# Attention over 128 heads on one core: engine programs rewritten as loops, and V's second unit multiplied one block later

## The chip, the core and the metric

The kernel runs on one core of a Trainium2 chip. A core has a matrix engine (TensorE, PE in the profile), a vector engine (VectorE, DVE), an activation engine (ScalarE, ACT), a general engine (GpSimd, POOL) and a queue engine for transfers (SyncE, SP), each with an instruction stream of its own; they meet only through semaphores. Sixteen DMA engines move data between HBM and the on-chip memory SBUF. Matmul results land in PSUM. The metric is the time of one execution on the device in microseconds (us), as the median of several runs.

## What is computed

Plain softmax attention with few queries and many keys, in bfloat16:

```python
B, H, Sq, Skv, Dh = 8, 16, 16, 2048, 256
scores = einsum('bhqd,bhkd->bhqk', q, k) * Dh ** -0.5
attn = softmax(scores)
out = einsum('bhqk,bhkd->bhqd', attn, v)
```

There are 128 heads (8 x 16), each with 16 queries and 2048 keys of 256 elements. K and V have 134 MB each, q and the output 1 MB each. Every byte of K and V is read once, so the kernel moves 270 MB.

## The kernel before, in words

**Blocks and units.** The 128 heads are taken in G = 16 blocks of 8 heads. A block has two units (e = 0 and 1) of K and two of V. A unit is 4 heads: 8192 rows of 256, laid out as 128 partitions x 64 rows x 256 elements, 4 MB, loaded with one DMA. SBUF holds four unit slots in the tensor `SL`, called KA, KB, VA and VB.

**Work of a block.** DVE transposes each K unit in place, in 32 x 32 squares of 4-byte words, so that the contraction lies on the partitions (`on_vector`, L154; four transposes a unit). PE then multiplies q with K: `qk` (L234 and L235, the helper `mm`; 16 matmuls of 512 columns for each half of a unit, 64 for a block) adds up scores of both units in the four PSUM banks of `S_ps`. The stationary operand is `QW`, a block-diagonal copy of the scaled queries that ACT writes for each block (`qwb`, L174). DVE takes the maximum over all 2048 scores (L156), ACT the exponentials in two halves with their sums (L206, into `P_sb`), DVE transposes these into `PTc` (L162, two halves) and computes the reciprocal of the sum (L164, L166). ACT copies `PTc` into `PTz` (L219), a tensor that is zero outside the diagonal squares: eight copies, four for each unit. PE multiplies `PTz` with V (`pv`, L251: 64 matmuls of 256 columns per unit, each with a weight load of its own), in a PSUM bank of its own for each unit. ACT evacuates each unit's 64 rows with the reciprocal as scale (`evac`, L180) and issues the store of the block's 128 output rows (L184).

**Order.** All loads go through SP (`load`, L97; the q load at L100), in the order K of block 0, K of block 1, V of block 0, K of block 2, V of block 1 and so on, K one block ahead of V. K of block 0 goes into the V slots, which are free then. A load of K waits until QK of the block before has read that slot (semaphores `c_qk`), a load of V until PV of the block before has (`c_pv`). PE runs in each round: QK of block g, then both PV units of block g-1; a wait on `c_cp` says that `PTz` of that block is written. ACT runs in each round: `QW` for the next block, the exponentials, evacuation and store of the block before last, then the eight copies. DVE runs K transposes, maximum, the transposes into `PTc`, sums, then the K transposes of the next block. At the end the last V units go into the K slots, in pieces that get smaller (`TAIL_A`, `TAIL`), so that PV can begin before the whole unit has landed.

**Programs.** PE's rounds 1 to 15 are one hardware loop whose body is written out (about 350 instructions with fixed addresses; only its semaphore thresholds come from the loop's register). The programs of SP, ACT and DVE are written out for all 16 blocks.

Of the kernel before, what the change touches and what calls it, by code (L numbers as in the profile page):

```python
# [7 lines left out]
PE = mybir.EngineType.PE  # L8
BF16 = mybir.dt.bfloat16
F32 = mybir.dt.float32  # L10

T = 64
KA, KB, VA, VB = 0, 1, 2, 3


def bass_standalone__softmax_full_bidir__sampling_kernel(
# [17 lines left out]
    qh = q.rearrange("b h s d -> (b h) (s d)")  # L34
    oh = out.rearrange("b h s d -> (b h s) d")

    with ExitStack() as es:
# [5 lines left out]
        PTc = ec(nc.sbuf_tensor("PTc", [128, T, 32], BF16))  # L43
        PTz = ec(nc.sbuf_tensor("PTz", [128, 2, T, 128], BF16))
        O_fin = ec(nc.sbuf_tensor("O_fin", [128, 2, D], BF16))
        negm = ec(nc.sbuf_tensor("negm", [128, G], F32))
        lsum = ec(nc.sbuf_tensor("lsum", [128, G, 2], F32))
        ltot = ec(nc.sbuf_tensor("ltot", [128, G], F32))
        rinv = ec(nc.sbuf_tensor("rinv", [128, G], F32))

        S_ps = ec(nc.psum_tensor("S_ps", [128, 4, 512], F32))
        O_ps = ec(nc.psum_tensor("O_ps", [128, 4, 512], F32))
# [4 lines left out]
        s_q = sem("s_q")  # L57
        s_k = [sem("s_ka"), sem("s_kb")]
        s_k0 = [sem("s_k0a"), sem("s_k0b")]
        s_v = [sem("s_va"), sem("s_vb")]  # L60
        s_st = [sem("s_st%d" % i) for i in range(2)]
        s_fin = sem("s_fin")
        c_pool = sem("c_pool")
        c_qt = sem("c_qt")
        c_qw = sem("c_qw")
        c_kt = [[sem("c_kt%d%d" % (e, h)) for h in range(2)] for e in range(2)]
        c_qk = [sem("c_qka"), sem("c_qkb")]
# [5 lines left out]
        c_pv = [sem("c_pv0"), sem("c_pv1")]  # L73
        c_pl = sem("c_pl")
# [4 lines left out]
        def ap_of(t_ap, offset, dims):  # L79
            return bass.AP(tensor=t_ap.tensor, offset=offset, ap=[list(t_ap.ap[0])] + [list(d) for d in dims])  # L80


        TAIL = [(0, 19), (19, 14), (33, 10), (43, 7), (50, 5), (55, 4), (59, 3), (62, 2)]
        TAIL_A = [(0, 37), (37, 27)]
        s_tail = [sem("s_t%d" % i) for i in range(len(TAIL))]
        s_vl = [sem("s_vl%d" % i) for i in range(len(TAIL_A))]
        s_vc = sem("s_vc")
        s_kl = sem("s_kl")

        def obank(g, e):  # L90
            return e + (2 if g == last else 0)

        def kslot(g, e):
            return (VA, VB)[e] if g == 0 else (KA, KB)[e]
# [3 lines left out]

        def on_sync(eng):
            eng.dma_start(QT[:], qh).then_inc(s_q, 16)  # L100
            for e in range(2):
                load(eng, ku, 0, e, kslot(0, e), 0, T, s_k0[e])
            for g in range(1, G):
                for e in range(2):
                    if g >= 2:
                        eng.wait_ge(c_qk[e], g)
                    if (g, e) != (last, 1):
                        load(eng, ku, g, e, kslot(g, e), 0, T, s_k[e])
                    else:
                        load(eng, ku, g, e, kslot(g, e), 0, 32, s_k[e])  # L110
                        load(eng, ku, g, e, kslot(g, e), 32, 32, s_kl)
                w = g - 1
                for e in range(2):
                    if w:
                        eng.wait_ge(c_pv[e], w)
                    else:
                        eng.wait_ge(c_qk[e], 1)
                    if (w, e) != (last - 1, 1):
                        load(eng, vu, w, e, (VA, VB)[e], 0, T, s_v[e])
                        if e:  # L120
                            eng.sem_inc(s_vc, 16)
                    else:
                        load(eng, vu, w, e, VB, 0, 32, s_v[e])
                        load(eng, vu, w, e, VB, 32, 32, s_vc)

            eng.wait_ge(c_qk[0], G)
            for (a, n), s in zip(TAIL_A, s_vl):
                load(eng, vu, last, 0, KA, a, n, s)
            eng.wait_ge(c_qk[1], G)
            for (a, n), s in zip(TAIL, s_tail):  # L130
                load(eng, vu, last, 1, KB, a, n, s)
            eng.wait_ge(c_ev, 2 * last + 2)
            eng.dma_start(oh[128 * last:128 * last + 128, :], O_fin[:, last % 2, :]).then_inc(s_fin, 16)
            eng.wait_ge(s_fin, 16)

        def on_gpsimd(eng):
            eng.memset(PTz[:].rearrange("p a t c -> p (a t c)").bitcast(F32), 0.0).then_inc(c_pool, 1)  # L137

        def on_vector(eng):
# [4 lines left out]
            for g in range(G):  # L144
                for e in range(2):
                    for c in range(4):
                        if g == 0 and c == 0:
                            eng.wait_ge(s_k0[e], 16)
                        elif c == 0:
                            eng.wait_ge(s_k[e], 16 * g)  # L150
                        elif (g, e, c) == (last, 1, 2):
                            eng.wait_ge(s_kl, 16)
# [5 lines left out]
                for h in range(2):  # L158
                    eng.wait_ge(c_ex[h], g + 1)
                    if g and h == 0:  # L160
                        eng.wait_ge(c_cp, 8 * g)
# [6 lines left out]
        def on_scalar(eng):  # L168
# [29 lines left out]
            for g in range(G):  # L198
# [4 lines left out]
                if g:  # L203
                    eng.wait_ge(c_pt, 2 * g)
# [113 lines left out]
```

## Time and profile before

| what | value |
|---|---|
| time, median of 3 runs | 636.18 us (635.99 to 636.28) |
| the profiled execution | 636.1 us, of which its span (first to last instruction) 634.8 us |
| DVE busy | 365.2 us (58%), of it K transposes 284.2 |
| ACT busy | 214.8 us (34%), of it copies to `PTz` 134.9 |
| HBM read and written | 269.48 MB and 1.05 MB |
| mean transfer rate over the span | 426 GB/s |
| chain that ended last, by engine | DMA 58%, PE 23%, DVE 16%, ACT 2% |
| granted TensorE clock, mean | 0.917 |

The profile is of one execution. Busy shares are means over the whole span; the 40 slices show how they change over time. The profile names each instruction by its engine and by its line in the kernel (L154 is line 154 of the listing above), its operation and its tiles. "Idle before, releaser" says how long an engine waited ahead of an instruction, and what it waited for. The DMA issues are listed by line, with the time from issue to landing.

### The profile page before, as it was taken

How to read it: one execution, taken by the hardware profiler on the slowest of the kernel's cores; microseconds unless marked ns; L12 is line 12 of the kernel's file. 1: busy time of each engine (PE TensorE's matmuls, PEld its weight loads, DVE VectorE, ACT ScalarE, POOL GpSimd, SP SyncE). 2: the span in 40 equal slices, each digit the busy share in tenths (PEclk: the TensorE clock that was granted, in tenths of full speed). 3: DMA queues.
4: the chain of work that ended last, by engine and by line, in shares of the span. 5: the costliest groups of instructions: out<-in, count | busy, mean ns of one | idle time of the engine just before them, and what ended most of it. 6: DMA issues, size and time to landing. Idle time of an engine off the chain costs nothing.

```text
span 634.8 us, 6396 instructions
## 1 busy us (share of the span) xinstructions
PE 488.3 (77%) x3072; PEld 274.9 (43%) x2560; DVE 365.2 (58%) x210; ACT 214.8 (34%) x289; POOL 7.1 (1%) x5
## 2 busy tenths in 40 slices
PE   0738989595896958869597795967959689595998
PEld 0202828154271532716336262452724527144287
DVE  2968583763738546294562945739366393663830
ACT  1042252525035250342513325142252322524170
POOL 4000000000000000000000000000000000000000
PEclk9978999798997989969799797998979989798899
DMA  8999999999999999999999999999999999999997
GB/s 376 436 441 432 428 432 432 430 430 431 432 429 434 429 432 433 429 434 429 433 430 429 432 429 433 430 430 433 434 429 436 433 433 432 432 432 425 430 425 285
DMA packets 13113, 270.64 MB, mean 426 GB/s; under 512 B 1456, under 2 KB 3760, under 8 KB 4400
## 3 DMA queue, kind: packets, MB, share of 16 engines
q1 hardware_dynamic: 10944, 269.55, 98.8%
q10 hardware_dynamic: 2160, 0.98, 0.5%
q8 instruction: 3, 0.05, 0.0%
q14 instruction: 6, 0.05, 0.0%
HBM read 269.48 MB, written 1.05 MB: 426 GB/s over the span
## 4 chain that ended last, share of the span: by engine, by line
DMA 58%; PE 23%; DVE 16%; ACT 2%; issue 0%; SPq 0%
DMA SL<-in_k_dram 58%; DVE SL L154 15%; PE S_ps L234 11%; PE S_ps L235 10%; PE O_ps L251 2%; ACT PTz L219 1%; DVE PTc L162 1%; DVE negm L156 1%; ACT P_sb L206 0%; ACT O_fin L180 0%; SPq L97 0%; SPq L100 0%; DVE rinv L166 0%; DVE ltot L164 0%
## 5 line engine op out<-in xcount | busy, mean ns | idle before, releaser
L154 DVE STREAM_TRANSPOSE SL<-SL 128x2048 f32<-128x2048 f32 x128 | 284.2, 2279 | 157.9 <-DMA SL<-in_k_dram 157.9
L234 PE MATMUL S_ps<-SL,QW 128*128 128x512 bf16 x512 | 214.0, 418 | 143.5 <-DVE SL L154 143.3
L251 PE MATMUL O_ps<-SL,PTz 128*128 128x256 bf16 x2048 | 226.3, 273 | 0.9 <-ACT PTz L219 0.7
L234 PEld LDWEIGHTS S_ps<-SL,QW 128*128 128x128 bf16 x512 | 75.1, 147 | 326.6 <-issue 171.7
L251 PEld LDWEIGHTS O_ps<-SL,PTz 128*128 128x128 bf16 x2048 | 199.8, 98 | 30.9 <-issue 4.5
L235 PE MATMUL S_ps<-SL,QW 128*128 128x512 bf16 x512 | 212.5, 415 | 0.0
L219 ACT ACTIVATE PTz<-PTc 32x1024 bf16<-32x1024 bf16 x128 | 134.9, 1054 | 11.3 <-ACT O_fin L180 5.9
L174 ACT ACTIVATE QW<-QT 32x256 bf16<-32x256 bf16 x64 | 26.8, 419 | 243.3 <-PE S_ps L235 236.2
L156 DVE TENSOR_REDUCE negm<-S_ps 128x1 f32<-128x2048 f32 x16 | 36.7, 2292 | 61.4 <-PE S_ps L235 61.4
L180 ACT ACTIVATE O_fin<-O_ps,rinv 64x256 bf16<-64x256 f32 x32 | 15.0, 468 | 137.6 <-PE O_ps L251 137.5
L162 DVE STREAM_TRANSPOSE PTc<-P_sb 128x1024 bf16<-128x1024 bf16 x32 | 37.9, 1224 | 20.3 <-ACT P_sb L206 20.3
L206 ACT ACTIVATE P_sb<-S_ps,negm 128x1024 bf16<-128x1024 f32 x32 | 35.3, 1109 | 25.5 <-DVE negm L156 25.5
L137 POOL MEMSET PTz<- 128x8192 f32 x1 | 6.9, 6924 | 0.3 <-POOLq L303 0.3
L206 ACT ACTIVATION_READ_ACCUMULATOR P_sb<-S_ps,negm 128x1 f32 x32 | 6.3, 196 | 0.0
L143 DVE STREAM_TRANSPOSE QT<-QT 128x2048 f32<-128x2048 f32 x1 | 2.3, 2312 | 3.7 <-DMA QT<-in_q_dram 3.7
L166 DVE RECIPROCAL rinv<-ltot 128x1 f32<-128x1 f32 x16 | 2.6, 164 | 0.5
L164 DVE TENSOR_REDUCE ltot<-lsum 128x1 f32<-128x2 f32 x16 | 1.8, 112 | 0.0
L174 ACT ACT_TABLE_LOAD x1 | 1.3, 1283 | 0.7 <-PEq L303 0.7
L140 DVE MEMSET QW<- 128x1024 f32 x1 | 0.9, 912 | 1.0 <-PEq L303 1.0
L303 POOL MEMSET const-bfloat16-1.0<- 128x1 bf16 x1 | 0.1, 101 | 0.0
L303 POOL MEMSET const-uint8-127<- 128x1 uint8 x1 | 0.1, 101 | 0.0
L303 POOL MEMSET const-float32-0.0<- 128x1 f32 x1 | 0.1, 98 | 0.2 <-issue 0.2
(1 smaller groups left out, 0.1 us busy)
## 6 DMA issues: line engine op xcount, KB each, us to landing
SL<-in_k_dram SPq DMA_DIRECT2D x31, 4096.0 KB, 25.8
SL<-in_v_dram SPq DMA_DIRECT2D x29, 4096.0 KB, 29.1
SL<-in_k_dram SPq DMA_DIRECT2D x2, 2048.0 KB, 23.7
SL<-in_v_dram SPq DMA_DIRECT2D x2, 2048.0 KB, 29.2
SL<-in_v_dram SPq DMA_DIRECT2D x1, 2368.0 KB, 21.6
SL<-in_v_dram SPq DMA_DIRECT2D x1, 1728.0 KB, 25.4
SL<-in_v_dram SPq DMA_DIRECT2D x1, 1216.0 KB, 20.7
QT<-in_q_dram SPq DMA_DIRECT2D x1, 1024.0 KB, 4.9
```

What stands on the lines that cost most here:

```text
L137: eng.memset(PTz[:].rearrange("p a t c -> p (a t c)").bitcast(F32), 0.0).then_inc(c_pool, 1)
L154: eng.transpose(x, x).then_inc(c_kt[e][c // 2], 1)
L156: eng.tensor_reduce(out=negm[:, g:g + 1], in_=S_ps[:].rearrange("p c n -> p (c n)"), axis=AX.X, op=ALU.max, negate=True).then_inc(c_mx, 1)
L162: eng.transpose(PTc[:, 32 * h:32 * h + 32, :].rearrange("p t x -> p (t x)"), P_sb[:, 1024 * h:1024 * h + 1024]).then_inc(c_pt, 1)
L166: eng.reciprocal(rinv[:, g:g + 1], ltot[:, g:g + 1]).then_inc(c_ri, 1)
L174: eng.activation(ap_of(dv, dv.offset, [[1024 + 512, 2], [2, 64], [1, 2]]), ap_of(sv, sv.offset + 2 * (8 * r + a), [[8, 2], [64, 64], [1, 2]]),
L180: eng.activation(O_fin[rows, g % 2, :], O_ps[rows, obank(g, e), 0:D], ACTF.Copy, scale=rinv[rows, g:g + 1]).then_inc(c_ev, 1)
L206: eng.activation(P_sb[:, 1024 * h:1024 * h + 1024], S_ps[:, 2 * h:2 * h + 2, :].rearrange("p c n -> p (c n)"), ACTF.Exp, bias=negm[:, g:g ...
L219: eng.activation(PTz[32 * a:32 * a + 32, z, :, 64 * e + 16 * a:64 * e + 16 * a + 16], sv[:, :, 16 * (a % 2):16 * (a % 2) + 16], ACTF.Copy) ...
L234: return eng.matmul(dst, w, x, start=start, stop=stop)
L235: return eng.add_instruction(mybir.InstMatmult(name=nc.get_next_instruction_name(), engine=PE, start_tensor_calc=start, stop_tensor_calc=stop,
L251: ins = eng.matmul(O_ps[:, bank, 0:D], PTz[:, z, t, :], SL[:, slot, t, :], start=(t == 0), stop=(t == T - 1))
```

## The change

All five engine programs become loops over the blocks, with addresses and semaphore thresholds worked out in registers.

- **PE** has one loop over 18 rounds r. In a round it clears the four banks of `S_ps` with four matmuls of a zero tile `ZZ`, does QK of block r (two nested loops; a pass of the inner one is four matmuls), and then two V units: x = 0 is the *second* unit of block r-2, x = 1 the *first* unit of block r-1. Both units of a block are added up in the same PSUM bank `O_ps`, which a zeroing matmul clears ahead of the first one, after the evacuation of the block before (`c_ev`). PV is a loop over four passes of 16 matmuls; it waits for the copies (`c_cp`) and for V (`c_vl`).
- **PTz** no longer holds both units of a block in one square; its two squares are one for each e.
- **ACT** in round g: `QW` for the next block, exponentials, evacuation of block g-2 (one instruction of 128 rows, after the second unit's PV), the four copies of block g-1's second unit, the store, then, after the transposes of block g, the four copies of block g's first unit.
- **DVE** transposes K by half units of 128 x 4096 words. Its transposes into `PTc` wait until the copies of the block before's second unit are done (`c_cp >= 8g + 9`).
- **SP** loads in a round: both K units of block j, V's second unit of block j-2, V's first unit of block j-1. K of the last block thus stands one V unit earlier in the queue. The last V units stay in the V slots, in pieces (`PIECES`), and wait for PV passes that free the slot piece by piece.
- **POOL** passes on the landing of V to PE (`c_vl`), and sets starting values of semaphores.
- **q** is loaded with its rows in another order: the source is viewed as `(u a) n -> a u n` with a = 4.

The core of the diff:

```diff
-KA, KB, VA, VB = 0, 1, 2, 3
+VA, VB, KA, KB = 0, 1, 2, 3
...
-    qh = q.rearrange("b h s d -> (b h) (s d)")
+    qh = q.rearrange("b h s d -> (b h) (s d)").rearrange("(u a) n -> a u n", a=4)
...
+        def k_and_v(eng, j, es):
+            for e in range(2):
+                eng.wait_ge(c_qk, 16 * j + 8 * e - 8)
+                load(eng, ku, j, e, KA + e, 0, T, s_k[e])
+            for e in es:
+                w = j - 1 - e
+                eng.wait_ge(c_pv, 8 * w + 4 * e + 4)
+                load(eng, vu, w, e, VA + e, 0, T, s_v[e])
...
+            for j in range(2, 3):
+                k_and_v(eng, j, (0,))
+            with nc.Fori(3, last, engines=[SP]) as j:
+                k_and_v(eng, j, (1, 0))
...
+            with nc.Fori(1, last, engines=[POOL]) as w:
                 for e in range(2):
+                    eng.wait_ge(s_v[e], 16 * w)
+                    eng.sem_inc(c_vl, T // C)
...
+            with nc.Fori(0, G, engines=[DVE]) as g:
+                eng.wait_ge(c_qk, 16 * g + 16)
+                eng.tensor_reduce(out=negm[:], in_=S_ps[:].rearrange("p c n -> p (c n)"),
                                   axis=AX.X, op=ALU.max, negate=True).then_inc(c_mx, 1)
                 for h in range(2):
+                    eng.wait_ge(c_ex[h], g + 1 + h)
+                    if h == 0:
+                        eng.wait_ge(c_cp, 8 * g + 9)
                     eng.transpose(PTc[:, 32 * h:32 * h + 32, :].rearrange("p t x -> p (t x)"),
                                   P_sb[:, 1024 * h:1024 * h + 1024]).then_inc(c_pt, 1)
...
+            with nc.Fori(0, G, engines=[ACT]) as g:
+                eng.wait_ge(c_qk, 16 * g + 16)
+                qwb((g + 1) & 15)
+                eng.wait_ge(c_mx, g + 1)
                 for h in range(2):
                     eng.activation(P_sb[:, 1024 * h:1024 * h + 1024],
                                    S_ps[:, 2 * h:2 * h + 2, :].rearrange("p c n -> p (c n)"), ACTF.Exp,
+                                   bias=negm[:], scale=1.0, accum_out=lsum[:, h:h + 1]).then_inc(c_ex[h], 1)
...
+                with eng.If_ne(g2, 0):
+                    evac(n)
+                with eng.If_ne(gg, 0):
+                    eng.wait_ge(c_pv, 8 * g)
+                    copies(1)
+                with eng.If_ne(g2, 0):
+                    store(n, (g + 14) & 15)
                 eng.wait_ge(c_pt, 2 * g + 2)
+                eng.wait_ge(c_pv, 8 * g + 4)
+                copies(0)
+            evac(last)
+            copies(1)
+            store(last, last - 1)
+            evac(G)
...
+            with nc.Fori(0, G + 2, engines=[PE]) as r:
+                rr = eng.to_reg(r)
+                with eng.If_lt(rr, G):
+                    slot = eng.snap(((r + 15) & 16) >> 3)
+                    eng.wait_ge(c_ex[1], r + 1)
+                    for c in range(4):
+                        mm(S_ps[:, c, :], ZZ[:, 0:128], ZZ[:], True, c == 0)
+                    with nc.Fori(0, 2, engines=[PE]) as e:
+                        for h in range(2):
+                            with nc.Fori(0, 4, engines=[PE]) as b:
+                                eng.wait_ge(c_kt, 4 * r + 2 * e + h + 1)
+                                for par in range(2):
+                                    for c in (2 * h, 2 * h + 1):
+                                        ins = mm(S_ps[:, c, :], QW[:, e, :, 2 * b + par],
+                                                 SLk[:, slot + e, c, :, b, :, par], False, c == 2 * h)
+                                ins.then_inc(c_qk, 1)
+                with nc.Fori(0, 2, engines=[PE]) as x:
+                    u = eng.snap(2 * r + x)
+                    valid = eng.to_reg((u + 29) & 32)
+                    with eng.If_ne(valid, 0):
+                        first = eng.to_reg(x)
+                        with eng.If_ne(first, 0):
+                            eng.wait_ge(c_ev, r)
+                            mm(O_ps[:, 0:D], ZZ[:, 0:128], ZZ[:, 0:D], True, True)
+                        base = eng.snap(4 - 4 * x)
+                        with nc.Fori(0, T // C, engines=[PE]) as c:
+                            eng.wait_ge(c_cp, 4 * u + 1)
+                            eng.wait_ge(c_vl, 4 * u + c + 1)
+                            for i in range(C):
+                                if i in INSIDE:
+                                    eng.wait_ge(INSIDE[i][1], 64 * u + 16 * c + 1)
+                                ins = mm(O_ps[:, 0:D], PTt[:, base + c, i, :], SLt[:, base + c, i, :], False, True)
+                            ins.then_inc(c_pv, 1)
```

280 lines of the change are left out of this document (114 added, 166 removed).

## The prediction

> **What bounds the kernel now.** I read the page's head first, then the DMA issues, then the timeline of DVE and of all engines for one late block, then the last stretch by windows.
>
> ```profile
> span 634.8 us, 6396 instructions
> ...
> PE 488.3 (77%) x3072; PEld 274.9 (43%) x2560; DVE 365.2 (58%) x210; ACT 214.8 (34%) x289; POOL 7.1 (1%) x5
> ...
> GB/s 376 436 441 432 428 432 432 430 430 431 432 429 434 429 432 433 429 434 429 433 430 429 432 429 433 430 430 433 434 429 436 433 433 432 432 432 425 430 425 285
> ...
> q1 hardware_dynamic: 10944, 269.55, 98.8%
> ...
> q8 instruction: 3, 0.05, 0.0%
> q14 instruction: 6, 0.05, 0.0%
> ...
> L206 ACT ACTIVATE P_sb<-S_ps,negm 128x1024 bf16<-128x1024 f32 x32 | 35.3, 1109 | 25.5 <-DVE negm L156 25.5
> ```
>
> The transfers are the limit. The SP queue (q1) holds 98.8% of the 16 engines' time, and the slices between the first and the last stay at 425 to 441 GB/s; only the first (376) and the last (285) fall off. PE's 77% is no limit here. Instruction fetch is nine packets, 0.10 MB: at 432 GB/s some 0.23 us of the transfers' time. Keeping programs resident can win no more than that.
>
> ```profile
> 504.41 8.89 DVE L154 STREAM_TRANSPOSE SL<-SL 128x2048 f32<-128x2048 f32 x4 [10.71 <-DMA SL<-in_k_dram]
> ...
> 543.41 8.89 DVE L154 STREAM_TRANSPOSE SL<-SL 128x2048 f32<-128x2048 f32 x4 [10.26 <-DMA SL<-in_k_dram]
> 553.25 8.89 DVE L154 STREAM_TRANSPOSE SL<-SL 128x2048 f32<-128x2048 f32 x4 [0.96 <-DMA SL<-in_k_dram]
> ...
> 569.54 2.37 DVE L162 STREAM_TRANSPOSE PTc<-P_sb 128x1024 bf16<-128x1024 bf16 x2 [1.27 <-ACT P_sb L206]
> ...
> 571.98 0.17 DVE L166 RECIPROCAL rinv<-ltot 128x1 f32<-128x1 f32 x1
> 582.41 17.66 DVE L154 STREAM_TRANSPOSE SL<-SL 128x2048 f32<-128x2048 f32 x8 [10.26 <-DMA SL<-in_k_dram]
> ```
>
> One block of eight heads lasts 39.0 us (504.41 to 543.41 to 582.41), which is four 4 MB units of 9.75 us. DVE ends a block at 572.15 and then idles 10.26 us, until the next K lands. So the chain of work inside a block takes 28.7 us, and the transfers give the pace.
>
> ```profile
> SL<-in_k_dram SPq DMA_DIRECT2D x31, 4096.0 KB, 25.8
> SL<-in_v_dram SPq DMA_DIRECT2D x29, 4096.0 KB, 29.1
> ...
> QT<-in_q_dram SPq DMA_DIRECT2D x1, 1024.0 KB, 4.9
> ```
>
> A K unit is issued 25.8 us before it lands, so about 16 us of older transfers are still ahead of it: every release may come some 16 us later before a DMA engine runs dry.
>
> ```profile
> 628.00:629.00 1.00, 1.00 (x11) 0.90 (x10) 0.00 (x0) 0.00 (x0) 0.00 (x0) 1.00 1.05 386
> 629.00:630.00 1.00, 1.00 (x11) 0.89 (x10) 0.00 (x0) 0.00 (x0) 0.00 (x0) 1.00 0.56 197
> 630.00:632.00 2.00, 2.00 (x21) 1.79 (x19) 0.00 (x0) 0.00 (x0) 0.00 (x0) 1.00 0.18 67
> ```
>
> The last two columns are the DMA engines' busy share and GB/s: the transfers end near 629.6 (0.56 of the slice at 629), the span at 634.8. At the end it is PE that is late:
>
> ```profile
> 565.78 14.13 PE L251 MATMUL O_ps<-SL,PTz 128*128 128x256 bf16 x128
> ...
> 573.05 0.47 ACT L180 ACTIVATE O_fin<-O_ps,rinv 64x256 bf16<-64x256 f32 x1 [2.44 <-PE O_ps L251]
> ...
> 580.84 8.60 ACT L219 ACTIVATE PTz<-PTc 32x1024 bf16<-32x1024 bf16 x8 [0.42 <-ACT O_fin L180]
> ...
> 603.71 14.13 PE L251 MATMUL O_ps<-SL,PTz 128*128 128x256 bf16 x128
> ...
> 632.71 0.47 ACT L180 ACTIVATE O_fin<-O_ps,rinv 64x256 bf16<-64x256 f32 x1 [6.44 <-PE O_ps L251]
> 633.21 0.35 SPq L133 DMA_DIRECT2D out_dram<-O_fin  x1
> ```
>
> PE begins its last 128 products only when the copies to PTz are done, and ends near 632.5; evacuation, store and its landing take the last 2.3 us. The execution's own time is 636.1 for a span of 634.8, so 1.3 us lie around it; the median is 636.18, 0.08 more. I sum against the span and add 1.4.
>
> **The change, part by part.** (a) *A serial chain through a block.* Today DVE transposes a block's probabilities as soon as the exponentials are there. Changed, this transpose waits (c_cp) for the four copies of the block before's second unit, ACT makes these behind an evacuation, and the evacuation waits for PV of the unit before that, which PE starts only after this block's QK. Behind the waiting transpose stand, on DVE, the sum, the reciprocal and the next block's K transposes, and for these QK waits, which frees the K slots; behind ACT's wait stand the copies and the store. So a block's period on DVE becomes: K transposes and QK, 565.78 - 543.41 = 22.37, less the 0.96 waited for the second K = 21.4; 64 products of p us each; hand-over, evacuation, restart 0.20 + 0.47 + 0.05; four copies, half of 8.60 = 4.30; hand-over 0.06, transposes 2.37, sum and reciprocal 0.3; six register or branch instructions in ACT's and DVE's loops 0.2. That is 29.35 + 64 p. With today's p = 14.13 / 128 = 0.110 it is 36.4, 2.6 below 39.0. The 10.3 us of cover shrink to that, and p decides.
>
> (b) *What a product costs when its addresses are in registers.* Each of the 64 steps becomes one instruction that works out addresses, a weight load and a matmul; per 16 steps come six more (waits, count, branch). No row shows such a step. From below it is 0.110, the array's own pace. From above: PE issues today's pair within 0.110, so 0.055 is the most an instruction of its sequencer takes now, and three with 6/16 more make 0.186. The only row that shows a sequencer's pace bare is POOL's start:
>
> ```profile
> 0.23 0.10 POOL L303 MEMSET const-float32-0.0<- 128x1 f32 x1 [0.23 <-issue]
> 0.27 0.10 POOL L303 MEMSET const-float32-1.0<- 128x1 f32 x1
> 0.30 0.10 POOL L303 MEMSET const-bfloat16-1.0<- 128x1 bf16 x1
> 0.34 0.10 POOL L303 MEMSET const-uint8-127<- 128x1 uint8 x1
> ```
>
> Four instructions start 0.11 / 3 = 0.037 us apart. By that row a step is 3 x 0.037 + 6/16 x 0.037 = 0.124, which I take: it is the one where nothing but issue sets the spacing. A pass of the QK loop, 17 instructions, is 0.63 and hides behind its four matmuls (16 of them end 3.6 us after the last K transposes, 0.9 for four). Then P = 37.3, still below 39.0.
>
> [...]
>
> (c) *The first blocks.*
>
> ```profile
> 15.34 8.89 DVE L154 STREAM_TRANSPOSE SL<-SL 128x2048 f32<-128x2048 f32 x4 [7.39 <-DMA SL<-in_k_dram]
> ...
> 43.87 17.64 DVE L154 STREAM_TRANSPOSE SL<-SL 128x2048 f32<-128x2048 f32 x8
> ...
> 68.90 2.37 DVE L162 STREAM_TRANSPOSE PTc<-P_sb 128x1024 bf16<-128x1024 bf16 x2 [1.27 <-ACT P_sb L206]
> ...
> 74.79 8.89 DVE L154 STREAM_TRANSPOSE SL<-SL 128x2048 f32<-128x2048 f32 x4 [3.28 <-DMA SL<-in_k_dram]
> ```
>
> Block 0 is as before, 28.5 us. In block 1 the transposes, which end with the sums at 68.90 + 2.37 + 0.3 = 71.6 today, come behind the second exponential (1.1, its group's mean) and four copies (4.3): 77.0, where K(2) landed at 74.8. K(3) comes a unit earlier than today, at 104.0, because one V unit is put off; DVE is there at 114.3, 10.3 late. That is within the 16 us, and the lag falls by 1.7 a block and is gone at block 10. It stays to the end if 77.0 + 13 P passes K(15)'s landing, 582.4 - 9.75 = 572.7: from P = 38.1, that is p = 0.137.
>
> (d) *The end.* K(15) lands 9.75 earlier. K start to PV start is 603.71 - 582.41 = 21.3, so PE begins at 594.0. Then come five V units in one line, 320 p, with two waits for an evacuation of 0.85 each (hand-over, 0.47, restart, the zeroing matmul), and 2.3 for evacuation and store: 598.0 + 320 p. At 0.110 it gives 633.2, 1.6 less than today; at 0.124 it gives 637.7. The V pieces land before PE needs them (the last near 629.6).
>
> (e) *The q load.* Its source is now read as 4 x 32 x 4096, its destination as 128 rows. Today all loads lead with 128 on both sides: the 10944 packets of q1 are 76 transfers of 128 rows and 16 completions each, so a transfer is dealt to 16 engines by its leading dimension. If 4 is what can be dealt, four engines carry q's 1.05 MB: 0.262 MB each instead of 0.066, at 432 / 16 = 27 GB/s 7.3 us more. Bounds: 0 (still 16 engines) and 36 us (one). I take four, since the leading 4 is what the instruction carries. These four then stay 7.3 us behind: every unit is spread over all 16, its release waits for the slowest, and nothing in a saturated stream lets them catch up. So all landings move by 7.3.
>
> [...]
>
> (f) *At nothing.* The zeroing of S_ps (four matmuls a block) and the rest of PE's loop lie in PE's idle time ahead of the K transposes; if the cover went, about 1 us a block. One evacuation of 128 rows takes the place of two of 64. POOL's passing on of V's landing is hidden as long as PE is later than V. Register addresses on SP hold up four issues in 39 us.
>
> Sum: 598.0 + 39.7 + 7.3 = 645.0; with 1.4 around it, 646.4.
>
> **The rivals.** *Slow issue on PE.* At the upper end, p = 0.186, P is 29.35 + 11.9 + 0.25 for QK = 41.5, DVE never catches up, and the end is 77.0 + 13 x 41.5 + 7.3 + 21.6 + 59.5 + 4.0 = 708.9, a time of 710. For it: a register address must be fetched, which no row of today contains. Against it: POOL's 0.037. It begins at p = 0.137.
>
> [...]
>
> *Not slower.* The q load is still dealt to 16 engines and the queue ahead of PE hides the address instructions, so p = 0.110: 598.0 + 35.2 + 1.4 = 634.6. For it: PE's queue runs ahead today, there is no gap between QK and PV at 565.78. Against it: the leading 4. With the split right and p = 0.110 it is 641.9; with 16 engines and p = 0.124 it is 639.1.
>
> *The programs do not stay resident.* Fetches would then show as instruction packets; one of today's nine is 0.011 MB, 0.03 us of the transfers, so it would take some forty more to be seen in the time. Against it: the loops are far shorter than today's programs.
>
> **How the numbers follow.** The forecast's case (four engines for q, p from 0.110 to 0.137, 642 to 652) gets 0.38; q on 16 engines with such p, 634.6 to 643, 0.15; slow issue, 652 to 740, 0.30; PE as the bound, above 740, 0.14; something not seen, 0.03. The likeliest is 646.4. The range runs from 634.5 to 740: it leaves out PE as the bound and little below. A measurement of this kernel can tell about 0.2%, 1.3 us: faster than 634.9 is only the good half of the third case, 0.08; within it 0.05; slower 0.87.
>
> **What would show it.** Right: q lands about 12 us after its issue instead of 4.9, and the first K transposes start near 22.6; 64 products of a V unit take 7.9 us; DVE waits for K again in the late blocks, 39.0 apart; the last five V units run on PE in one line. Wrong: products 0.14 us apart or more, DVE's K transposes released by its own chain, and middle slices below 425 GB/s (slow issue); PE busy without a gap all through (PE as the bound); q landing after 5 us (the split). If steps cost 0.124 but hand-overs in the chain cost over 0.8 us more than counted, the lag of block 3 would stay and my sum would be short by 13 times the excess.

## The result and the profile after

The changed kernel takes **1011.63 us** (median, 1011.02 to 1012.06), against 636.12 (635.99 to 636.28) in the same comparison: 1.590 times, 95% interval 1.588 to 1.593. The direction was forecast, the size was not: 646.4 was the likeliest value, and 1011 lies far above the range's upper end of 740.

From the page of the changed kernel: the span, the transfers by slice and queue, the chain by engine, the two costliest groups of PE instructions, and the issue of a K unit:

```profile
span 1009.4 us, 13539 instructions
...
GB/s 164 407 325 188 287 299 262 273 332 252 270 314 270 265 299 299 253 282 313 251 280 325 270 252 312 292 242 300 313 251 273 319 263 268 316 273 62 239 265 3
...
q1 hardware_dynamic: 11220, 269.55, 67.6%
...
q14 instruction: 1, 0.01, 0.0%
...
PE 41%; issue 27%; DVE 20%; ACT 5%; DMA 5%; ACTq 1%; DVEq 0%; SPq 0%
...
L273 PE MATMUL O_ps<-SL,PTz 128*128 x2048 | 362.5, 298 | 100.0 <-issue 85.5
L273 PE MATMUL S_ps<-SL,QW 128*128 x512 | 215.1, 420 | 165.3 <-issue 142.2
...
SL<-in_k_dram SPq DMA_DIRECT2D x31, 4096.0 KB, 12.2
```

The transfers no longer set the pace: q1 is at 67.6% where it stood at 98.8%, and the middle slices (the 5th to the 36th) lie between 242 and 332 GB/s. A K unit lands 12.2 us after its issue instead of 25.8, and 4 MB took 9.75 us in the full stream, so little is left in the queue when a load comes. The chain is PE and "issue", 68% together; "issue" is time in which an engine waited for nothing that the profile shows. The two groups say that much of it is PE's: ahead of the products and of QK's matmuls PE idled 85.5 and 142.2 us with "issue" as the reason. Instruction packets went from nine to one (0.10 MB to 0.01), so the programs do stay resident (hardly any instructions are fetched while it runs), and by transfer time that alone is worth next to nothing.

DVE's timeline gives the stages (start, busy time, and idle time ahead with what ended it):

```profile
29.89 2.31 DVE L175 STREAM_TRANSPOSE QT<-QT 128x2048 f32<-128x2048 f32 x1 [27.95 <-DMA QT<-in_q_dram]
39.32 8.77 DVE L179 STREAM_TRANSPOSE SL<-SL 128x4096 f32<-128x4096 f32 x2 [7.12 <-DMA SL<-in_k_dram]
...
476.72 17.42 DVE L179 STREAM_TRANSPOSE SL<-SL 128x4096 f32<-128x4096 f32 x4
513.70 2.29 DVE L187 TENSOR_REDUCE negm<-S_ps 128x1 f32<-128x2048 f32 x1 [19.56 <-PE S_ps L274]
533.62 2.37 DVE L194 STREAM_TRANSPOSE PTc<-P_sb 128x1024 bf16<-128x1024 bf16 x2 [17.63 <-ACT PTz L232]
...
536.28 17.43 DVE L179 STREAM_TRANSPOSE SL<-SL 128x4096 f32<-128x4096 f32 x4
...
893.62 17.42 DVE L179 STREAM_TRANSPOSE SL<-SL 128x4096 f32<-128x4096 f32 x4
```

The first K transposes start at 39.32 (15.34 before), one block lasts 536.28 - 476.72 = 59.56 (39.0 before), and block 15 starts at 893.62, from where it is 115.8 to the end (52.4 from 582.41 before). So the 374.6 us that the span grew are +24.0 ahead of block 0, +287.2 over the 15 blocks in between, and +63.4 in the last. In this block, DVE waits 19.56 for QK and 17.63 for the copies, not for K.

PE's timeline of one block (passes of the QK loop first, from 486.05; PV passes of 16 steps from 515.11):

```profile
487.80 0.44 PE L273 MATMUL S_ps<-SL,QW 128*128 x1 [0.66 <-issue]
...
489.56 0.44 PE L273 MATMUL S_ps<-SL,QW 128*128 x1 [0.65 <-issue]
...
491.31 0.44 PE L273 MATMUL S_ps<-SL,QW 128*128 x1 [0.66 <-issue]
...
515.11 6.35 PE L273 MATMUL O_ps<-SL,PTz 128*128 x32 [1.45 <-issue]
522.24 2.81 PE L273 MATMUL O_ps<-SL,PTz 128*128 x16 [0.79 <-issue]
525.79 2.78 PE L273 MATMUL O_ps<-SL,PTz 128*128 x16 [0.74 <-issue]
...
544.51 0.39 PE L273 MATMUL S_ps<-ZZ 128*128 128x512 bf16 x1 [0.92 <-issue]
```

In this block PE has no break longer than 1.45 us. A QK pass of four matmuls starts every 1.755 us (487.80, 489.56, 491.31), though its four matmuls, 0.22 apart, need 0.9 at the array's pace; 16 of them with their loop ends take 515.11 - 486.05 = 29.1. A PV pass of 16 steps starts every 3.55 (522.24 to 525.79): 16 steps in 2.78 to 2.81, 0.174 each, and about 0.75 "issue" at the pass's end. Both V units with the zeroing matmul take 544.51 - 515.11 = 29.4, the clearing ahead of QK 1.1. That is the whole of 59.6.

What PE's sequencer (its register, ALU and branch instructions are the PEldq rows of these views) does in between stands in three answers on single lines. L273 is the helper's matmul, L291 the QK loop, L307 the PV loop; the columns after the count are the least, median and largest duration in ns:

```profile
L273 PEldq FUSED_REGOPS  x2816: 74/74/195, 44.0 to 1006.8; - x188
...
L273 PEldq ALU_OP  x1024: 32/36/36, 43.8 to 1004.4; - x171
```
```profile
L291 PEldq COMPARE_BRANCH  x256: 76/208/219, 45.1 to 930.1; - x128
```
```profile
L307 PEldq COMPARE_BRANCH  x128: 76/208/209, 116.1 to 1007.1; - x128
```

The 2816 register operations of L273 come to about one of 74 ns for each of its 2560 steps of a weight load and a matmul (2048 of PV, 512 of QK); ALU operations of 36 stand besides. In both loops three of four branches are taken, and in both a quarter took 76 ns (64 of the 256, 32 of the 128) and the others 207 to 219: so 208 goes with the taken branch and 76 with the one that leaves the loop. 0.174 for a step less 0.074 leaves 0.10 for the weight load and the matmul; that the three run one after the other is assumed here, no row shows it.

### The profile page after: what moved, and what is told of

Read it like the earlier page. It is cut to its first block, busy times and chain, and to the rows that moved or that the text cites. A ratio compares the mean times of both kernels' runs of the same rounds, so it can differ in the third digit from the quotient of the medians.

```text
span 1009.4 us, 13539 instructions
## 1 busy us (share of the span) xinstructions
PE 675.5 (67%) x3152; PEld 281.9 (28%) x2592; DVE 359.3 (36%) x146; ACT 208.8 (21%) x277; POOL 7.7 (1%) x6
## 3 DMA queue, kind: packets, MB, share of 16 engines
q1 hardware_dynamic: 11220, 269.55, 67.6%
## 4 chain that ended last, share of the span: by engine, by line
PE 41%; issue 27%; DVE 20%; ACT 5%; DMA 5%; ACTq 1%; DVEq 0%; SPq 0%
PE O_ps L273 20%; DVE SL L179 18%; PE S_ps L273 12%; PE S_ps L274 9%; ACT PTz L232 5%; DMA SL<-in_k_dram 5%; DVE PTc L194 2%; ACTq L237 1%; DVE negm L187 0%; DVEq L185 0%; ACT O_fin L225 0%; ACTq L236 0%; ACT P_sb L247 0%; DVE rinv L198 0%; ACTq L225 0%
## 5 line engine op out<-in xcount | busy, mean ns | idle before, releaser
L273 PE MATMUL O_ps<-SL,PTz 128*128 x2048 | 362.5, 298 | 100.0 <-issue 85.5
L273 PE MATMUL S_ps<-SL,QW 128*128 x512 | 215.1, 420 | 165.3 <-issue 142.2
L179 DVE STREAM_TRANSPOSE SL<-SL 128x4096 f32<-128x4096 f32 x64 | 278.9, 4414 | 8.1 <-DMA SL<-in_k_dram 8.1
L273 PEld LDWEIGHTS O_ps<-SL,PTz 128*128 x2048 | 204.7, 100 | 262.7 <-issue 151.4
L274 PE MATMUL S_ps<-SL,QW 128*128 x512 | 202.1, 395 | 0.0
L273 PEld LDWEIGHTS S_ps<-SL,QW 128*128 x512 | 74.1, 145 | 389.6 <-issue 389.6
L219 ACT ACTIVATE QW<-QT 32x256 bf16 (+1 forms) x68 | 28.3, 416 | 456.7 <-PE S_ps L274 425.2
L225 ACT ACTIVATE O_fin<-O_ps,rinv 128x256 f32 (+1 forms) x16 | 7.6, 473 | 184.4 <-PE O_ps L273 184.4
L273 PE MATMUL S_ps<-ZZ 128*128 128x512 bf16 x16 | 6.6, 415 | 52.1 <-ACT QW L219 34.5
L273 PEld LDWEIGHTS S_ps<-ZZ 128*128 128x128 bf16 x16 | 1.5, 97 | 55.2 <-issue 50.0
L274 PE MATMUL S_ps<-ZZ 128*128 128x512 bf16 x48 | 14.3, 411 | 0.0
L273 PE MATMUL O_ps<-ZZ 128*128 128x256 bf16 x16 | 4.6, 284 | 14.4 <-ACT O_fin L225 12.9
L273 PEld LDWEIGHTS O_ps<-ZZ 128*128 128x128 bf16 x16 | 1.5, 96 | 17.6 <-ACT O_fin L225 15.6
L198 DVE RECIPROCAL rinv<-ltot 128x1 f32 x16 | 2.6, 164 | 2.1
## 6 DMA issues: line engine op xcount, KB each, us to landing
SL<-in_k_dram SPq DMA_DIRECT2D x31, 4096.0 KB, 12.2
```

Of the source, the lines that this page charges most:

```text
L179: eng.transpose(x, x).then_inc(c_kt, 1)
L198: eng.reciprocal(rinv[:, bass.ds(g + 1, 1)], ltot[:]).then_inc(c_ri, 1)
L219: eng.activation(dv, sv, ACTF.Copy, scale=scale).then_inc(c_qw, 1)
L225: eng.activation(O_fin[:, n, :], O_ps[:, 0:D], ACTF.Copy, scale=rinv[:, bass.ds(n, 1)]).then_inc(c_ev, 1)
L273: return eng.matmul(dst, w, x, start=start, stop=False, skip_group_check=True)
L274: return eng.add_instruction(mybir.InstMatmult(name=nc.get_next_instruction_name(), engine=PE, start_tensor_calc=start, stop_tensor_calc=F ...
```

## The experiments

My theory after the result ("Theory 1" in the expectations): PE's instruction stream with register addresses is the bound, and the q load costs a fixed delay at the start; the rest of the change costs nothing that can be seen. The rivals: the new order itself (the serial chain, one accumulation for both units, PV a block later) makes the kernel slow; or loop ends, not addresses, do.

### PE written out, everything else changed

```diff
-            with nc.Fori(0, G + 2, engines=[PE]) as r:
...
-                            with nc.Fori(0, 4, engines=[PE]) as b:
...
-                        with nc.Fori(0, T // C, engines=[PE]) as c:
...
+            qk(0, VA)
+            qk(1, KA)
+            pv(1, 1)
+            with nc.Fori(2, G, engines=[PE]) as r:
+                qk(r, KA)
+                pv(r, 0)
+                pv(r, 1)
+            pv(G, 0)
+            pv(G, 1)
+            pv(G + 1, 0, True)
```

`qk` and `pv` hold the same matmuls with fixed addresses; only the loop over the rounds is left.

> The changed kernel with PE's inner loops written out (fixed addresses, one loop over the rounds); order, waits, semaphores and the q load stay as changed. Theory 1, PE's sequencer cannot issue register-addressed products fast enough: blocks are 39.0 us apart again, transfers give the pace, and only the late q load stays: 633.2 + 24.0 for the later first K + about 1.4 = 659 us. Theory 2, the new serial chain (V's second unit one block later, copies ahead of the transposes) is itself what is too long: DVE's period stays well above 39, above 750 us.

Measured: 660.79 us (659.75 to 661.29), 1.039 times before (1.038 to 1.041). Its DVE timeline:

```profile
39.33 8.77 DVE L179 STREAM_TRANSPOSE SL<-SL 128x4096 f32<-128x4096 f32 x2 [7.15 <-DMA SL<-in_k_dram]
...
557.07 8.77 DVE L179 STREAM_TRANSPOSE SL<-SL 128x4096 f32<-128x4096 f32 x2 [1.93 <-DMA SL<-in_k_dram]
...
596.08 17.42 DVE L179 STREAM_TRANSPOSE SL<-SL 128x4096 f32<-128x4096 f32 x4 [1.94 <-DMA SL<-in_k_dram]
```

Blocks are 39.0 us apart again (557.07 to 596.08), and DVE waits 1.93 for K ahead of each: the transfers are the bound. So 1011.63 - 660.79 = 350.8 of the 375.5 us come from PE's register addresses and loops, with the new order, the chain, the single bank and the later second unit all in place. What is left is the start: the first K at 39.33.

### One half written out at a time

```diff
 PV only:
+                for x in range(2):
+                    valid = eng.to_reg((2 * r + x + 29) & 32)
                     with eng.If_ne(valid, 0):
+                        pv(r, x)
 QK only:
                 with eng.If_lt(rr, G):
...
+                    qk(r, KA)
```

> The changed kernel with only PV written out (fixed addresses); QK stays a loop of passes with register addresses, everything else as changed. If QK's passes are slow by issue (1.755 us each, as in the changed kernel), a block is the serial chain: QK 28.1 from the first transposed half, PV 7.3, evacuation and copies 5.0, transposes and sums 2.8, first K half 4.4: about 48 us a block, 823 us. If PV's steps alone were the trouble: 39 us a block, about 660 us.

> The changed kernel with only QK written out; PV stays loops with register addresses (3.55 us for a pass of 16). If PV's steps are slow by issue: PE is the bound at about 46 us a block, near 800 us. If QK's passes alone were the trouble: 39 us a block, about 660 us.

PV written out: 821.95 (a single run), where 823 was expected; with QK's loop alone a block takes 48.1 (732.09 to 780.18 between two maxima on DVE). QK written out: 733.76 (a single run) where about 800 was expected, a miss: a block takes 41.1 (470.25 to 511.40 between two K transposes on DVE) and not 46. PE's timeline of it shows most of the difference:

```profile
493.42 3.65 PE L273 MATMUL O_ps<-SL,PTz 128*128 x32
497.36 2.80 PE L273 MATMUL O_ps<-SL,PTz 128*128 x16 [0.29 <-issue]
500.90 2.78 PE L273 MATMUL O_ps<-SL,PTz 128*128 x16 [0.74 <-issue]
```

The first 32 steps after QK take 3.65, 0.114 each, where two passes of 3.55 would take 7.1; only then the passes start every 3.5 us. I read this so: while QK's written-out matmuls keep the array busy, PE's sequencer works out the addresses of two passes ahead. The rows above do not hold the sequencer's own times, so that stays a reading. The two halves alone cost 161.2 and 73.0 us more than the 660.79, 234 together, where both cost 350.8. So they are not worth a fixed sum: one half alone still finds cover in a block of 39 us, and PV's first two passes behind written-out matmuls take 3.65 instead of 7.1.

### Steps or loop ends

```diff
-                        with nc.Fori(0, T // C, engines=[PE]) as c:
+                        for c in range(T // C):
```

All 64 steps of a unit stand in one pass, their addresses still in registers.

> The changed kernel with a V unit's 64 steps in one pass instead of four passes of 16; addresses stay in registers. It tells the loop's own cost from that of a step. If 0.74 us are lost at each pass's end and a step costs 0.174: a unit falls from 14.1 to 11.9 us, a block by 4.5 us, the time to about 940 us. If only the steps cost: about 1010 us.

Measured: 927.47 (a single run), somewhat below the 940. PE's timeline has the 64 steps of a unit in one piece:

```profile
482.42 11.06 PE L273 MATMUL O_ps<-SL,PTz 128*128 x64 [1.34 <-issue]
```

A block is 54.2 (806.23 to 860.42 between two maxima on DVE), 5.4 less without the eight loop ends, 0.67 each. A step takes 11.06 / 64 = 0.173, against 0.110 with fixed addresses, so the 128 steps of a block cost 8.1 us and their loop ends 5.4: more of PV's price is the steps, and the loop ends are real. This holds for PV only. QK's 16 passes take 29.1 where the array needs 16 x 0.9 = 14.4, and no run tells there how much of that is addresses and how much the end of a pass.

### Where the 24 us at the start come from

```diff
 the changed kernel, q in four loads:
-            eng.dma_start(QT[:], qh).then_inc(s_q, 16)
+            for a in range(4):
+                eng.dma_start(QT[32 * a:32 * a + 32, :], qh[a]).then_inc(s_q, 16)
...
-            eng.wait_ge(s_q, 16)
+            eng.wait_ge(s_q, 64)
 the kernel before, q in the changed view:
+    qh = q.rearrange("b h s d -> (b h) (s d)").rearrange("(u a) n -> a u n", a=4)
 the same, and nothing loaded beside q:
             eng.dma_start(QT[:], qh).then_inc(s_q, 16)
+            eng.wait_ge(s_q, 16)
 the kernel before, a view that leads with 16:
+    qh = q.rearrange("b h s d -> (b h) (s d)").rearrange("(u a) n -> a u n", a=16)
```

> The changed kernel with its q load cut in four loads of 32 rows each, so that each leads with 32 on both sides. Theory 1: q lands near 5 us, the first K transposes start near 15.5 instead of 39.3, everything else moves up by that: 1011.6 - 24.0 = 988 us. If the q load costs nothing once PE is the bound: 1011 us.

> The kernel before with nothing changed but the source view of the q load (rows in another order, so the heads' queries are mixed up). By what the changed kernel shows, the first K transposes start at 39.3 instead of 15.3 and nothing catches up: 636.1 + 24.0 = 660 us. By the prediction's split over four engines at full pace: 636.1 + 7.3 = 643.4 us. If the lateness of q in the changed kernel came from something else there: 636 us.

> As the run before, but SP waits until q has landed before it issues the first K load, so that q moves alone. If four engines move q at 27 GB/s each when nothing else is under way: q lands near 12 us and the first K transposes start near 23: about 644 us. If the four engines are slow by themselves (9 GB/s each): q still lands near 29 and the first K transposes start near 40: about 661 us.

> The kernel before with q's source viewed as 16 x 8 rows instead of 4 x 32 (rows in another order, so the heads' queries are mixed up). If it is the leading 4 that confines q to four engines: with 16 q lands within 5 to 8 us and the time is 636 to 639 us. If it is the three-dimensional source or the order of rows: q still lands near 30, 661 us.

Measured: 989.32 for the changed kernel with q in four loads (1.556 times before, 1.553 to 1.558), with the first K at 17.40; and 661.12 (a single run) for the kernel before with nothing but the view:

```profile
40.11 8.89 DVE L154 STREAM_TRANSPOSE SL<-SL 128x2048 f32<-128x2048 f32 x4 [7.07 <-DMA SL<-in_k_dram]
```

Both are near what was expected: the view alone moves the first K by 24.8 us and costs 25. With a leading 16, q's transpose and the first K on DVE come at

```profile
8.27 2.31 DVE L143 STREAM_TRANSPOSE QT<-QT 128x2048 f32<-128x2048 f32 x1 [6.34 <-DMA QT<-in_q_dram]
17.84 8.89 DVE L154 STREAM_TRANSPOSE SL<-SL 128x2048 f32<-128x2048 f32 x4 [7.26 <-DMA SL<-in_k_dram]
```

and the time is 638.6 (a single run), though the source has three dimensions as with 4. So it is the leading 4, not the shape; 2.5 us against the kernel before remain (q's transpose was at 5.64 there), and why is not shown. The packets agree: in the changed kernel 11220 on q1 are 78 transfers of 128 rows and 16 completions, 11232, less 12, so q has four completions. With q in four loads (at the head of SP's queue, below) they are 11280, 60 more: 4 x (32 + 16) = 192 in place of 128 + 4 = 132.

The run with nothing beside q was to tell whether four engines are slow by themselves (29) or only in company (12). It fell between: DVE's transpose of q begins at 20.70, and the time is 653.67 us (a single run). Two stretches of the start of this run, then two of the changed kernel (the last two columns are the mean busy share of 16 DMA engines and GB/s):

```profile
4.00:8.00 4.00, 0.00 (x0) 0.00 (x0) 0.00 (x0) 0.00 (x0) 3.65 (x1) 1.00 0.24 57
...
12.00:16.00 4.00, 0.00 (x0) 0.00 (x0) 0.00 (x0) 0.00 (x0) 0.00 (x0) 1.00 0.26 66
```
```profile
12.00:16.00 4.00, 0.00 (x0) 0.00 (x0) 0.00 (x0) 0.00 (x0) 0.00 (x0) 1.00 0.89 139
16.00:20.00 4.00, 0.00 (x0) 0.00 (x0) 0.00 (x0) 0.00 (x0) 0.00 (x0) 1.00 1.34 209
```

Alone, the busy share is a quarter (0.24 to 0.26), as of four engines out of 16, and 57 to 66 GB/s pass, 14 to 16 for each of the four; in the kernel before 16 engines move 432, 27 each. In company the share is 0.89 and more, and yet only 139 to 209 GB/s pass in all. So the four engines move q at about half the pace (14 to 16 instead of 27), and in company q and K are slower together (139 to 209 in all instead of 432). The prediction had q there at about 12.7; alone it is there 8.0 later, in company (29.89) another 9.2, and with the 7.3 that were forecast this makes about the 24. Why both paces fall is open: no run here varied the size of these packets or their place.

### The rest of the change, with its price taken away

```diff
 PE written out, q in four loads on ACT's queue:
+            for a in range(4):
+                eng.dma_start(QT[32 * a:32 * a + 32, :], qh[a]).then_inc(s_q, 16)
 PE written out, q in four loads at the head of SP's queue:
-            eng.dma_start(QT[:], qh).then_inc(s_q, 16)
+            for a in range(4):
+                eng.dma_start(QT[32 * a:32 * a + 32, :], qh[a]).then_inc(s_q, 16)
             for g, s0, s in ((0, VA, s_k0), (1, KA, s_k)):
 PE written out, the four loads of q behind the first K unit:
                 for e in range(2):
                     load(eng, ku, g, e, s0 + e, 0, T, s[e])
+                    if g == 0 and e == 0:
+                        for a in range(4):
+                            eng.dma_start(QT[32 * a:32 * a + 32, :], qh[a]).then_inc(s_q, 16)
```

> The changed order with PE's inner loops written out, and q loaded in four loads of 32 rows by ACT's queue beside the first K. By the prediction's sum at 0.110 us a step and q on all engines: first K at 15.3, 39.0 us a block, the end at 633.2, a time of 634.6 us, 1.5 less than the kernel before. If the longer chain costs something by itself even with PE at full pace: 638 us or more.

> Changed kernel with PE's inner loops written out, and q loaded in four transfers of 32 rows at the head of SP's queue. With PE's loops left as changed this q load brought the first K 21.9 us forward (39.32 to 17.40), and took 22.3 us off the time. If the two causes add, the written-out kernel's 660.79 falls by the same: 638.9. If the late start was partly caught up in the run with written-out loops, the gain is smaller: 640 to 650.

> Changed kernel with PE's inner loops written out, and q loaded in four transfers of 32 rows that stand on SP's queue behind the first K unit and not ahead of it; DVE transposes the first K unit before q. If the price of the change is only PE's register addresses and the split of the q load to four engines, nothing is left of it here: the first K transposes start near 13 us, and the time is what the prediction's sum gave for the case not slower, 634.6, or, by the run with q on ACT's queue (646.45, first K 10.6 us late), 646.45 - 10.6 = 635.9: the same as before within 0.3%. Rival: the chain through a block and the longer row of V products at the end cost something of their own, some 2 to 5 us: 638 to 641.

**On ACT's queue:** 646.45 (645.99 to 646.66), 1.016 times before (1.015 to 1.018); 634.6 was expected. The q load, which is under way beside K there (320 to 393 GB/s in all from 4 to 20 us), is there for DVE only at 23.69, and the first K transposes start at 25.93, 10.6 later than before. That is the miss: 634.6 + 10.6 = 645.2, so the rest of the sum held to 1.3.

**At the head of SP's queue:** 639.07 (637.85 to 639.49), 1.005 times before (1.003 to 1.006). 660.79 - 639.07 = 21.7, where the same split took 22.3 off with PE's loops in place (1011.63 - 989.32): the two causes add. Its DVE timeline and the products of its last stretch:

```profile
17.27 8.77 DVE L180 STREAM_TRANSPOSE SL<-SL 128x4096 f32<-128x4096 f32 x2 [7.37 <-DMA SL<-in_k_dram]
...
39.58 2.29 DVE L188 TENSOR_REDUCE negm<-S_ps 128x1 f32<-128x2048 f32 x1 [3.84 <-PE S_ps L275]
...
114.72 17.43 DVE L180 STREAM_TRANSPOSE SL<-SL 128x4096 f32<-128x4096 f32 x4
...
150.65 17.43 DVE L180 STREAM_TRANSPOSE SL<-SL 128x4096 f32<-128x4096 f32 x4
...
535.21 8.77 DVE L180 STREAM_TRANSPOSE SL<-SL 128x4096 f32<-128x4096 f32 x2 [1.96 <-DMA SL<-in_k_dram]
...
```
```profile
L274 PE MATMUL O_ps<-SL,PTz x320: 269/273/283, 595.6 to 633.8; 128*128 128x256 bf16 x160
...
  POOLq L166: 2.0, 4
```

In the early blocks, while K is there in time, DVE's chain takes 150.65 - 114.72 = 35.93 a block, and late in the kernel it waits 1.96 for K. Of the 320 products at the end the first starts at 595.6 and the last at 633.8, with 2.0 us of waits for the last pieces of V, which POOL passes on (POOLq L166).

**Behind the first K unit:** 642.66 (641.76 to 643.64), 1.011 times before (1.009 to 1.012), a miss: 634.6 to 635.9 was expected, or 638 to 641. Its DVE timeline at the start, and two stretches by windows:

```profile
13.75 8.77 DVE L179 STREAM_TRANSPOSE SL<-SL 128x4096 f32<-128x4096 f32 x2 [11.81 <-DMA SL<-in_k_dram]
...
43.78 2.29 DVE L190 TENSOR_REDUCE negm<-S_ps 128x1 f32<-128x2048 f32 x1 [7.12 <-PE S_ps L277]
```
```profile
92.00:96.00 4.00, 4.00 (x19) 1.32 (x9) 4.00 (x2) 0.00 (x0) 0.00 (x0) 0.96 0.65 279
96.00:100.00 4.00, 4.00 (x20) 1.29 (x9) 4.00 (x2) 0.00 (x0) 0.00 (x0) 1.00 0.51 147
```

The first K transposes start at 13.75 as expected, but DVE turns to q only behind the first K unit (at 22.45), QK of block 0 waits for that, and the maximum starts at 43.78 instead of 39.58. The slots come free about four us later, and the queue runs dry once: DMA is busy for 0.65 and 0.51 of two stretches of 4 us. That is 3.4 us lost, nearly all of the 3.6 by which this run is slower than the one with q first. In the two slices of the page around them (80 to 112 us) 395 and 363 GB/s pass; with q first no slice from 16 to 127 us falls below 427. Neither theory had the cover of the first blocks right; it is thinner than later. So no version here beats the kernel before.

### The same register steps in the old order

```diff
+            def pvr(e, slot):
+                eng.matmul(O_ps[:, e, 0:D], ZZ[:, 0:128], ZZ[:], start=True, stop=False)
+                with nc.Fori(0, 4, engines=[PE]) as c:
+                    for i in range(16):
+                        eng.matmul(O_ps[:, e, 0:D], PTt[:, 0, c, i, :], SLt[:, slot, c, i, :],
+                                   start=False, stop=False, skip_group_check=True)
...
-                    pv(e, (VA, VB)[e], 0, e, 32 * e, T).then_inc(c_pv[e], 1)
+                    pvr(e, (VA, VB)[e]).then_inc(c_pv[e], 1)
```

The kernel before, with PV of blocks 0 to 14 as register-addressed loops and QK as it was.

> The kernel before, in its own order, with the PV of blocks 0 to 14 as loops of four passes of 16 steps with register addresses (with a zeroing and a closing matmul of a zero tile for each unit); QK stays written out. Theory 1: PE has QK 14 and PV 28.6 a block and becomes the bound at about 44.5 us a block: about 712 us. If the changed order (the serial chain) were needed for the loss: 39 us a block, 636 to 640 us.

Measured: 643.53 against 636.07 (a single run of each): neither the 712 nor the 636 to 640. PE's timeline of one block:

```profile
487.50 6.06 PE L258 MATMUL O_ps<-SL,PTz 128*128 x48
493.93 2.62 PE L258 MATMUL O_ps<-SL,PTz 128*128 x16 [0.37 <-issue]
...
499.94 2.62 PE L258 MATMUL O_ps<-SL,PTz 128*128 x16 [0.34 <-issue]
502.90 2.62 PE L258 MATMUL O_ps<-SL,PTz 128*128 x16 [0.34 <-issue]
```

48 steps pass at 0.126 each, the later passes start every 2.96, and PV of a block takes 21 us instead of 14 and not the 28.6 expected. With QK's 14 PE has 35 of the 39.0 us to do and is not the bound: DVE's K transposes stay 39.0 apart (426.11 to 465.10) with a wait of 10.34 for K, and 7 us more on PE are hidden in every block. The loss of 7.5 us lies at the end. The last 128 products, which are written out as before, start 7.4 later; here they are, first in this run, then in the kernel before:

```profile
625.97 14.13 PE L264 MATMUL O_ps<-SL,PTz 128*128 128x256 bf16 x128
```
```profile
618.53 14.15 PE L251 MATMUL O_ps<-SL,PTz 128*128 128x256 bf16 x128 [0.69 <-ACT PTz L219]
```

So in this run the price counted only where no cover was left. The run is not a plain copy of the changed kernel's PV: its passes hold no waits and end with 0.34 of "issue" instead of 0.74. So the 7.5 here and the 73.0 for looped PV in the changed order can't be set side by side as the price of the order, and no run has QK's loops in the old order.

## Why the prediction was wrong, point by point

**What bounds the kernel before:** right. Transfers, with cover for the chain; the kernel with the changed order and PE at full pace is bound by them again (639.07).

**(a) The chain:** right. 29.35 + 64 p gave 36.4 at p = 0.110; measured 35.93. With PE at full pace the chain costs nothing in the late blocks, as said.

**(b) A step with register addresses: this is the step that failed.** I took three instructions at POOL's spacing of 0.037 each, 0.124 with the loop's share, and 0.186 as the upper end. Measured: 0.074 for the register operation, by difference 0.10 for weight load and matmul, and about 0.75 at the end of each pass, 3.55 / 16 = 0.222 in all. The upper end rested on "PE issues today's pair within 0.110, so 0.055 is the most an instruction of its sequencer takes now"; but an instruction that works with registers is not one that issues a matmul: by the rows it takes 0.074. In the same step "A pass of the QK loop, 17 instructions, is 0.63 and hides behind its four matmuls" failed worse: 1.755, against 0.9 that could hide it. QK's passes alone, with PV at full pace and q late, make 822, 161 more than with both written out.

The prediction called POOL's start the only row that shows a sequencer's pace bare. That reading was wrong: PE's one loop of the kernel before, at L266, has rows of its own.

```profile
L266 PEldq COMPARE_BRANCH  x16: 76/208/309, 34.1 to 615.8; - x16
L266 PEldq FUSED_REGOPS  x15: 44/44/44, 34.5 to 578.2; - x15
L266 PEldq ALU_OP  x15: 36/36/36, 77.2 to 615.7; - x15
```

They show no address, but they price a register operation on PE at 44 ns and the end of a pass at 208 + 36. As an estimate from them, with nothing overlapping, a pass of 16 steps is 16 x (0.110 + 0.044) + 0.24 = 2.7 us, 0.169 a step. That is past the 0.137 from which the prediction's own sum leaves the transfers' pace. It is still below the 0.222 measured.

**(c) The first blocks, (d) the end:** confirmed where they can be seen without the two mis-sized terms, in the run with q at the head of SP's queue. Block 1 ends there 61.5 us after the first K transposes (78.79 - 17.27), where 77.0 - 15.34 = 61.7 was forecast, and the page's slices from 16 to 127 us all lie between 427 and 440 GB/s: the lag is hidden. The end comes 636.3 us into the span of the profiled execution (637.85, the fastest of five), against 633.2 in the sum at p = 0.110. The later start (17.27 - 15.34 = 1.9) and the waits for V pieces that I had in time (2.0) make 3.9 of which 3.1 are seen. The run with q behind K shows that the cover of the first blocks is thin: 4.2 us more of lag there were not hidden.

**(e) The q load:** the mechanism, four engines by the leading 4, was right by what the runs show (four completions, a busy share of 0.24 to 0.26 alone, 638.6 us with 16 where 4 gave 661.12); the size, 7.3, was 24.0. I had priced the four engines at the saturated pace of 27 GB/s each, and assumed that the others keep theirs. Both assumptions were off: 14 to 16 for each engine alone, and 139 to 209 GB/s in all in company.

**The rivals.** That PE itself becomes the bound (above 740, chance 0.14) is what happened: PE has no break over 1.45 us in the block shown, and DVE's K transposes follow its own chain. In measured terms the 16 QK passes, the 128 steps and the hand-overs are 16 x 1.755 + 128 x 0.222 + 3.1 = 59.6 a block (the 3.1 are what is left, 1.1 of them the clearing). So the mechanism had a name and a chance, and the range was cut below it. The pace per instruction that I took for this case is shown by no run; what the runs show in its place is 0.222 for a step, 1.755 for a QK pass, 0.074 for the register operation and by difference 0.10 for weight load and matmul together. POOL's 0.037 was a poor guide to PE.

**Residency:** as said, next to nothing: eight packets fewer. By transfer time the gain that the loops could bring was 0.2 us; the price of those on PE was 351.

In sum: 350.8 for PE's loops, 21.7 for the q load and 3.0 for the rest make 375.5. These are steps from run to run, so they add up by construction; that the first two are independent rests on the 22.3 and 21.7 for the q load.

## What to carry to other kernels

Price an instruction of a loop from rows of the same engine: ask the trace for the line of any loop that the engine already has. Where it has no row that computes an address, no upper bound follows from the pace of fixed-address instructions (here 0.055 was taken from it, and the register operation alone took 0.074), and the range must reach to the case in which that engine becomes the bound. Count what an engine issues per pass against what its array needs per pass: here a pass of four matmuls (0.9 us of array) did not hide its addresses and its end (1.755), while two or three passes behind written-out matmuls ran at nearly full pace (0.114 and 0.126 a step against 0.110). Before changing the view of a load, look at its leading dimension, and look at the start of the trace for what the loads behind it do.

## What the runs showed of the hardware

- On PE a register operation ahead of a register-addressed step takes 74 ns (medians of 46 to 123 on other lines), an ALU operation 32 to 36, a compare-and-branch of the two inner loops 208 at the median. A quarter of these, as many as leave the loops, take 76, the others 207 to 219.
- Behind written-out matmuls of QK, 32 register-addressed steps in one kernel and 48 in another ran at 0.114 and 0.126 us before the pace inside a pass fell to 0.175 and 0.164. PE's sequencer working ahead of a busy array is the reading of this; its own times there are not shown.
- The q load with a leading 4 (four completions) moves 57 to 66 GB/s alone at a busy share of 0.24 to 0.26, 14 to 16 for each of four engines; beside K units' transfers 139 to 209 GB/s pass in all.
- Four q loads of 32 rows are there for DVE at 7.59 us from the head of SP's queue and at 23.69 from ACT's queue beside K's loads: a second queue did not get them ahead.
